# Moving loads, transposes and score bursts around in a fused attention and feed-forward kernel

## The chip, the cores and the metric

The kernel runs on one core of a Trainium2 chip. The metric is the device time of one execution in microseconds (us); lower is better. Before the change the median of 11 runs is 532.79 us (530.18 to 536.34).

## What is computed

For each of 8 batches and 12 heads, with 448 tokens and 64 features per head, an attention without softmax: the scaled scores are cut at zero, squared and divided by the length. The heads of a token are put side by side into a row x of 768 features. Each row is normalised (mean and variance over the row, a gain per feature), goes through two matrices with a cut at zero between them, and is added to x.

```python
scores = scale * np.matmul(q, k.transpose(0, 1, 3, 2))
attn = np.maximum(scores, 0.0) ** 2 / S
x = np.matmul(attn, v)                       # heads side by side: (8, 448, 768)
mu, var = x.mean(-1), ((x - mu) ** 2).mean(-1)
xn = (x - mu) / np.sqrt(var + 1e-06) * g_ln
out = x + np.maximum(xn @ w_ch1, 0.0) @ w_ch2    # 768 -> 3072 -> 768
```

## The kernel before

The order of all instructions on each engine is written out by hand (`tc.manual_schedule`): each engine works through its own list in program order, and semaphores between the lists keep data right. So an instruction that waits holds up all that follow it on its engine.

**Work items.** Heads go in pairs; pair i belongs to batch i // 6, so pairs 12 to 17 are batch 2. A pair's q and k are turned so that features lie on partitions: for batches 0 and 1 on TensorE (`pe_T`), for batches 2 to 7 by a transposing DMA (`att_T`, L253) out of a ring of three slots, `qk_ring`, which `load_qk` (L160) fills with three GpSimd-issued loads. `load_v` (L170) loads the values of two pairs. `att_QK` (L268) computes scores for 128 keys of both heads of a pair and cuts them at zero into a tile `at`; `att_square` (L294) squares them on VectorE. A pair has three such score steps. The last 64 keys of two neighbouring pairs are taken together in a fourth step of the even pair (t == NF, L279), which therefore reads the turned q and k of both pairs. `att_AV` (L304) multiplies by the values and evicts the result to `xT`, which has two halves of 448 columns, used by even and odd batches in turn; the eviction is on VectorE (L326), or, while FFN1 of batch 1 runs, on ScalarE (L324).

**Stages.** Batch 0's attention comes first (`step_fine`, `first_end`). Then, for each batch b: FFN1 (`ffn_1_all`: 24 columns of 128 hidden units, each 12 matmuls at L397 and a relu at L399 on ScalarE, with two PSUM banks in turn), then FFN2. FFN2 of batch 0 is plain (`ffn_2_first`, L442); the later ones form the product of 2 x 2 blocks from seven products with sums of blocks (`seven`, L459). The sums of weight blocks that this needs are made on VectorE (L210), some in FFN2 of batch 0 and the rest in FFN1 of batch 1.

**Bursts.** Between FFN1 columns of batch b stand the scores of batch b + 1: `excursion(3)` first multiplies a finished pair by its values, then issues three score steps. For batch 1 and on, these stand after the columns in `IN_REST` (1, 4, ... 19), and after column 22 the last pair is multiplied by its values. When a pair's last score step is issued, `queued` puts the transposing DMA of the pair three later on SyncE's queue, and notes the load of the pair six later.

**Normalisation.** The gain is applied to `xT` into `xc` (on ScalarE; for the first `GAIN_FIRST` parts of batch 0 on VectorE, L331), and the mean is taken off afterwards. For batch 0 the mean comes from `mean_part` (L340), six TensorE products with a matrix of -1/768; in `ffn_1_first` a part whose gain was applied on VectorE gets its mean with one VectorE instruction (`center_part`, L363), the others with an addition (L661) and a ScalarE scaling (L662). The division by the standard deviation is left to the end of FFN2.

**Tokens in rows.** For the residual addition and the variance, `ffn_x` (L373) copies x to `x_tok`, with tokens on partitions, by a transposing DMA for each sixth of the features. Tokens are taken in tiles of 128 over the batch borders: batch 0 has tiles 0 to 2, batch 1 tiles 3 to 6. Batch 1's transposes therefore start at column 384 of `xT`, 64 columns inside the half that batch 0 used and that batch 2 uses next. `ffn_stats` (L386) takes mean and variance of a tile on VectorE.

**Queues.** SyncE issues all transposing DMAs and all stores (L421), in program order. GpSimd issues all loads but the first few.

Of the kernel before, what the change touches and what calls it, by code (L numbers as in the profile page):

```python
# [11 lines left out]
def kernel(  # L12
# [29 lines left out]
    K1 = d_model // P  # L42
    K2 = d_ff // P
# [116 lines left out]
    def load_qk(i):  # L160
        b, a = divmod(i, NPAIR)
        ring = qk_ring[:, i % 3]
        q_to = ring[:SP, :NJ].rearrange("p j (x d) -> p j x d", x=2)
        k_to = ring[:, NJ:].rearrange("p t (x d) -> p t x d", x=2)
        heads = slice(2 * a, 2 * a + 2)
        nc.gpsimd.dma_start(q_to, q[b, heads].rearrange("x (p j) d -> p j x d", j=NJ))  # L166
        nc.gpsimd.dma_start(k_to[:, :NF], k[b, heads, :SF].rearrange("x (p t) d -> p t x d", t=NF))  # L167
        nc.gpsimd.dma_start(k_to[:SS, NF], k[b, 2 * a:2 * a + 2, SF:].rearrange("x s d -> s x d"))  # L168

    def load_v(i):  # L170

        b, a = divmod(i, NPAIR)
        v_heads, v_rest = v_parts(b)
        nc.gpsimd.dma_start(v_heads[:, 2 * a:2 * a + 4],
                            v[b, 2 * a:2 * a + 4, :SF].rearrange("h (p t) d -> p h (t d)", t=NF))
        for r0, h0, step in ((0, 0, 3), (D, 1, 1)):
            heads = slice(h0, h0 + step + 1, step)
            nc.gpsimd.dma_start(v_rest[r0:r0 + SS, a:a + 2, r0:r0 + D],  # L178
                                v[b, 2 * a:2 * a + 4][heads, SF:].rearrange("h s d -> s h d"))
# [88 lines left out]
    def att_QK(i, t, relu_by=nc.scalar):  # L268

        at = attn_pool.tile([P, 2, S], bf16, tag="attn")  # L270
        attn[i, t] = at
        ps = next_sc() if relu_by is nc.scalar else None
        half = [bank[:, :S] for bank in (spare if ps is None else (ps[:, 0], ps[:, 1]))]
        if t == NF:
            for x in range(2):
                for hh in range(2):
                    r = slice(hh * D, (hh + 1) * D)
                    r0 = row0(i + x, hh)
                    nc.tensor.matmul(by_j(half[x][r0:r0 + SS]), k_of(i + x, r, t, SS), q_of(i + x, r),  # L279
                                     start=True, stop=True)  # L280
        else:
            for hh in range(2):
                r = slice(hh * D, (hh + 1) * D)
                nc.tensor.matmul(by_j(half[hh]), k_of(i, r, t, P), q_of(i, r), start=True, stop=True)  # L284
        if ps is None:
            for x in range(2):
                if relu_by[x] is nc.scalar:
                    nc.scalar.activation(at[:, x], half[x], Act.Relu)
                else:
                    nc.vector.tensor_scalar(at[:, x], half[x], 0.0, None, op0=Alu.max)  # L290
        else:
            nc.scalar.activation(at, ps[:, :, :S], Act.Relu)  # L292
# [2 lines left out]
        nc.vector.tensor_mul(attn[i, t], attn[i, t], attn[i, t])  # L295


    GAIN_FIRST = 2
    av = {}

    def xT_of(b, ki):
# [2 lines left out]
    def att_AV(i, half=None, bank=None, evac_by=None):  # L304
# [24 lines left out]
        if b == 0:  # L329
            if pr < GAIN_FIRST:  # L330
                nc.vector.tensor_scalar(xc[:, pr, :], xT_of(b, pr), g_sb[:, pr:pr + 1], None, op0=Alu.mult)  # L331
# [7 lines left out]
    def mean_part(ki):  # L339
        nc.tensor.matmul(mean0, ones, xT_of(0, ki), start=(ki == 0), stop=(ki == K1 - 1))  # L340
# [218 lines left out]
    def warm_up(n):  # L559
        for _ in range(n):  # L560
            nc.tensor.matmul(spare[1][:, :256], ones, warm, start=True, stop=True)
# [47 lines left out]
    def step_fine(i):  # L609

        att_QK(i, 0)
        att_T(i + 1)
        att_square(i, 0)
        att_QK(i, 1)
        att_square(i, 1)
        if i:
            att_AV(i - 1, 0)
        else:
            warm_up(3)
        att_QK(i, 2)  # L620
        if i:
            att_AV(i - 1, 1)
        else:
            warm_up(3)
        att_square(i, 2)
        att_QK(i, NF)
        att_square(i, NF)
        if i:
            mean_part(i - 2)
            warm_up(1)  # L630
        else:
            warm_up(3)
        att_QK(i + 1, 0)
        if i:
            mean_part(i - 1)
        att_T(i + 2)
        att_square(i + 1, 0)
        att_QK(i + 1, 1)
        att_square(i + 1, 1)
        att_AV(i, 0)  # L640
        att_QK(i + 1, 2)
        att_AV(i, 1)
        att_square(i + 1, 2)

    def first_end():
        i = NPAIR
        att_AV(i - 1, 0)
        att_QK(i, 0)
        mean_part(i - 2)
        att_QK(i, 1)  # L650
        att_AV(i - 1, 1)
        mean_part(i - 1)

# [21 lines left out]
    T_IN_FIRST = {4: 1, 7: 2, 10: 3, 13: 4, 16: 5}  # L675
    X_AT = (4, 6, 8, 10, 12, 14)
    V_AT = {21: PE_T * NPAIR + 2, 23: PE_T * NPAIR + 4}
    STATS_AT = {0: (18, 21, 23), 1: (20, 21, 22, 23), 2: (6, 9, 12, 15)}
    IN_REST = (1, 4, 7, 10, 13, 16, 19)

    def ffn_1_all(b):
        ms = tiles_of(b)
        for ni in range(NI0 if b == 0 else 0, K2):
            if b == 0 and ni == NI0:
                ffn_1_first()
            if b < 2 and ni in X_AT:
                ffn_x(b, X_AT.index(ni))
            if b == 0 and ni in V_AT:
                load_v(V_AT[ni])
            ffn_1(ni)  # L690
            flush()
            at = STATS_AT[min(b, 2)][:len(ms)]
            if ni in at:
                ffn_stats(ms[at.index(ni)])
            if b == 1 and ni in SUMS_AT:
                w2_sums(*LATE_SUMS[SUMS_AT.index(ni)])
            if b == 0:
                if ni in IN_FIRST:
                    excursion(3)
                if ni == IN_FIRST[-1] + 3:  # L700
                    next_AV(bank=spare[1])
                if ni in T_IN_FIRST:
                    att_T(NPAIR + T_IN_FIRST[ni])
            elif b < B - 1:
                if ni in IN_REST:
                    excursion(3, **(dict(third=(nc.scalar, nc.vector), evac_by=nc.scalar) if b == 1 else {}))
                if ni == IN_REST[-1] + 3:
                    flush_loads()
                    next_AV(bank=spare[1])

# [5 lines left out]
    def ffn_2_first():  # L716
        b = 0
        ffn_rstd(b)
        box = {}
        assert not ready  # L720
        steps = center(1)
        n = 0
        for dh in range(2):

            order = [(m, part) for m in range(2) for part in range(4)]
            if dh:
                order.sort(key=lambda x: x[1] // 2)
            for m, part in order:
                plain_part(b, m, dh, part, 4, box)
                if n < K1 - 1:  # L730
                    gain(1, n)
                if n == 3:
                    gain(1, K1 - 1)
                if n in CENTER_AT:
                    steps[CENTER_AT.index(n)]()
                if n == 8:
                    carry(b)
                if n in (9, 10):
                    w2_sums(B_TOP, B11, B12, Alu.add, n - 9)
                if n in (12, 13):  # L740
                    w2_sums(B_SUM, B11, B22, Alu.add, n - 12)
                n += 1
# [33 lines left out]
    with tc.manual_schedule(engines=set(ENGINES)):  # L776
        load_heads(0, [("q", 2, 2), ("k", 2, 2), ("k last", 2, H - 2), ("q", 4, 4), ("k", 4, 4), ("v", 0, 4),
                       ("v last", 0, H), ("q", 8, 4), ("k", 8, 4), ("v", 4, 4), ("v", 8, 4)])
        load_early()
        load_heads(1, [("q", 0, 2), ("k", 0, 2), ("k last", 0, H)])  # L780
        load_w1(0)
        load_heads(1, [("q", 2, 4), ("k", 2, 4)])
        load_w1(1)
        load_w1(2)
        load_heads(1, [("v", 0, H), ("v last", 0, H), ("q", 6, 6), ("k", 6, 6)])
        for c in range(3, NCH):
            load_w1(c)
        warm_up(17)
        att_T(0)
        warm_up(5)  # L790
        for i in range(0, NPAIR, 2):
            step_fine(i)
        first_end()
        load_w2(B11, 0, 0)
        load_w2(B21, 1, 0)
        load_w2(B12, 0, 1)
        load_w2(B22, 1, 1)
        nc.gpsimd.memset(qk_ring, 0.0)
        i = PE_T * NPAIR
        load_qk(i)  # L800
        load_qk(i + 1)
        load_v(i)
        load_qk(i + 2)
        for b in range(B):
            ffn_1_all(b)
            if b == 0:
                ffn_2_first()
            else:
                ffn_2_all(b)
        flush()  # L810
# [30 lines left out]
```

## Time and profile before

| what | value |
|---|---|
| median of 11 runs | 532.79 us |
| profiled execution, its own time | 533.93 us |
| its span, first to last instruction | 532.2 us |
| granted TensorE clock, mean | 0.992 |
| TensorE matmuls (PE) busy | 519.9 us, 98% |
| VectorE (DVE) | 374.8 us, 70% |
| ScalarE (ACT) | 273.5 us, 51% |
| GpSimd (POOL) | 221.5 us, 42% |
| batch 0's attention | 4.7 to 28.3 us |
| FFN1 of batch 0 | 29.1 to 70.0 us |
| FFN2 of batch 0 | 70.0 to 86.0 us |
| FFN1 of batch 1 | 86.0 to 132.3 us |
| FFN1 of batch 2 | 160.0 to 197.8 us |

Times in the profile are counted from the first instruction. A busy share says how long an engine was at work, not that it held the others up; for that one reads who waited for whom. SP is SyncE, which only issues DMAs; the time from its issue to the landing of the data is given beside an issue's line. The granted clock is the share of full speed at which TensorE was allowed to run.

### The profile page before, as it was taken

Reading aid. Unit: us, or ns where it says so; the run is one execution under the profiler, and the core shown is the slowest. Engines: PE = TensorE matmul, PEld = TensorE weight load, DVE = VectorE, ACT = ScalarE, POOL = GpSimd, SP = SyncE. Lnnn points to the kernel's source line nnn. Section 1 sums busy time; section 2 is a strip of 40 time slices with the busy share of each in tenths; the row PEclk is TensorE's granted clock in tenths of the full one; section 3 lists DMA queues with packets and bytes.
Section 4 is the critical chain, followed back from the end, with each engine's and each line's share of the span. In section 5 each row is a group of like instructions: output and inputs, shape, how many; then the busy total and the mean of one; then the engine's idle time right before and its main releaser. Section 6 shows DMA issues by size and latency. Waiting matters only on the chain.

```text
span 532.2 us, 13700 instructions
## 1 busy us (share of the span) xinstructions
PE 519.9 (98%) x5707; PEld 315.1 (59%) x5707; DVE 374.8 (70%) x661; ACT 273.5 (51%) x445; POOL 221.5 (42%) x255
## 2 busy tenths in 40 slices
PE   8989999799999999999999999999999999999996
PEld 4345566355885556655566556655666556665665
DVE  5957779466876868669785787789685886951165
ACT  6965643566326663176632766376623666234320
POOL 8618116665433573425743256627732000320021
PEclk9999999889999999999999999999999999999999
DMA  9999999999534995549953599969914210240022
GB/s 141 175 186 205 203 198 122 193 124 120 51 82 91 106 115 51 105 95 111 98 66 89 91 104 105 127 76 106 115 46 108 53 21 2 59 115 10 1 60 61
DMA packets 175230, 53.04 MB, mean 100 GB/s; under 512 B 154176, under 2 KB 175168, under 8 KB 175168
## 3 DMA queue, kind: packets, MB, share of 16 engines
q0 software_dynamic: 103552, 25.74, 54.8%
q1 hardware_dynamic: 71088, 26.06, 27.6%
q8 instruction: 44, 0.72, 0.6%
q10 hardware_dynamic: 528, 0.37, 0.2%
q14 instruction: 18, 0.15, 0.1%
HBM read 51.91 MB, written 11.01 MB: 118 GB/s over the span
## 4 chain that ended last, share of the span: by engine, by line
PE 79%; DMA 12%; POOL 4%; DVE 2%; issue 1%; ACT 1%; POOLq 0%; ACTq 0%; DVEq 0%
PE f L397 35%; PE f L459 33%; DMA qk_ring<-in_q_dram 6%; PE f L319 5%; DMA s_sb<-in_v_dram 4%; PE sc L284 3%; DMA x_tok<-xT 2%; PE f L284 1%; DMA out_dram<-o_t 1%; POOL w L201 1%; DVE w L210 1%; POOL w L141 1%; POOL w L144 1%; PE sc L279 1%; POOL w L206 1%
## 5 line engine op out<-in xcount | busy, mean ns | idle before, releaser
L397 PE MATMUL f<-xc,w 128*64 128x448 bf16 x2256 | 229.8, 356 | 4.2 <-ACT xT L324 3.5
L397 PEld LDWEIGHTS <-w 128*64 128x64 bf16 x2256 | 125.9, 110 | 99.0 <-issue 23.3
L399 ACT ACTIVATE h<-f 128x448 bf16<-128x448 f32 x188 | 102.7, 546 | 104.6 <-PE f L397 103.1
L459 PE MATMUL f<-w,s_sb 128*64 128x384 bf16 (+2 forms) x1584 | 130.0, 324 | 0.0
L459 PEld LDWEIGHTS <-s_sb 128*64 128x64 bf16 x1584 | 92.3, 110 | 35.0
L292 ACT ACTIVATE at<-sc 128x896 bf16<-128x896 f32 x120 | 103.2, 916 | 16.0 <-PE sc L284 13.1
L295 DVE TENSOR_TENSOR at<-at 128x896 bf16<-128x896 bf16 x168 | 95.7, 616 | 10.1 <-ACT at L292 9.9
L493 POOL TENSOR_TENSOR o_t<-o_t,x_tok 128x384 f32<-128x384 f32 x26 | 24.4, 939 | 153.0 <-ACT o_t L492 138.6
L166 POOL DMA_DIRECT2D qk_ring<-in_q_dram x36 | 45.0, 1250 | 90.6 <-DMA qkT_t<-qk_ring 79.9
L290 DVE TENSOR_SCALAR at<-f 128x448 bf16<-128x448 f32 x89 | 51.5, 617 | 23.2 <-PE f L284 23.2
L453 DVE TENSOR_TENSOR s_sb<-h 128x1536 bf16<-128x1536 bf16 x65 | 64.8, 1013 | 0.0
L492 ACT ACTIVATE o_t<-f,rstd 128x384 f32<-128x384 f32 x26 | 15.1, 581 | 93.2 <-DVE acc L497 45.3
L167 POOL DMA_DIRECT2D qk_ring<-in_k_dram x36 | 53.7, 1492 | 4.6 <-DMA w<-in_moe_w_ch_dram 4.6
L459 PE MATMUL f<-w,h 128*64 128x384 bf16 x624 | 52.9, 326 | 0.0
L168 POOL DMA_DIRECT2D qk_ring<-in_k_dram x36 | 45.0, 1250 | 5.7 <-DMA w<-in_moe_w_ch_dram 5.7
L326 DVE TENSOR_SCALAR xT<-f 128x448 bf16<-128x448 f32 x43 | 26.7, 621 | 28.7 <-PE f L319 26.7
L459 PEld LDWEIGHTS <-h 128*64 128x64 bf16 x624 | 36.6, 110 | 14.4
L319 PE MATMUL f<-at,v_ring 128*64 128x448 bf16 x336 | 40.7, 359 | 0.2 <-DMA v_ring<-in_v_dram 0.2
L493 POOL TENSOR_TENSOR acc<-acc,x_tok 128x384 f32<-128x384 f32 x24 | 28.1, 1177 | 22.5 <-ACT acc L492 22.5
L178 POOL DMA_DIRECT2D v_ring<-in_v_dram x36 | 31.6, 1159 | 5.2 <-DMA w<-in_moe_w_ch_dram 5.0
L363 DVE SCALAR_TENSOR_TENSOR xc<-f,g_sb,xc 128x448 bf16<-128x448 f32 x44 | 27.9, 677 | 6.4 <-PE f L356 6.0
L284 PE MATMUL sc<-qkT_t 64*128 64x448 bf16 x206 | 31.5, 356 | 0.0
(81 smaller groups left out, 381.2 us busy)
## 6 DMA issues: line engine op xcount, KB each, us to landing
w<-in_moe_w_ch_dram POOLq DMA_DIRECT2D x6, 768.0 KB, 13.2
w<-in_moe_w_ch_dram POOLq DMA_DIRECT2D x4, 1152.0 KB, 26.7
v_ring<-in_v_dram POOLq DMA_DIRECT2D x21, 192.0 KB, 5.4
qk_ring<-in_q_dram POOLq DMA_DIRECT2D x36, 112.0 KB, 4.5
qk_ring<-in_k_dram POOLq DMA_DIRECT2D x36, 96.0 KB, 5.2
out_dram<-o_t SPq DMA_DIRECT2D x9, 168.0 KB, 2.2
out_dram<-o_t SPq DMA_DIRECT2D x9, 144.0 KB, 2.1
out_dram<-acc SPq DMA_DIRECT2D x7, 144.0 KB, 2.0
```

What stands on the lines that cost most here:

```text
L166: nc.gpsimd.dma_start(q_to, q[b, heads].rearrange("x (p j) d -> p j x d", j=NJ))
L167: nc.gpsimd.dma_start(k_to[:, :NF], k[b, heads, :SF].rearrange("x (p t) d -> p t x d", t=NF))
L284: nc.tensor.matmul(by_j(half[hh]), k_of(i, r, t, P), q_of(i, r), start=True, stop=True)
L290: nc.vector.tensor_scalar(at[:, x], half[x], 0.0, None, op0=Alu.max)
L292: nc.scalar.activation(at, ps[:, :, :S], Act.Relu)
L295: nc.vector.tensor_mul(attn[i, t], attn[i, t], attn[i, t])
L319: nc.tensor.matmul(ps[hh * D:(hh + 1) * D, :], weights, values, start=(n == 0), stop=(n == NF))
L397: nc.tensor.matmul(ps[c * D:(c + 1) * D, :], w1[:, ki, n0:n0 + D], xc[:, ki, :], start=(ki == 0), stop=(ki == K1 - 1))
L399: nc.scalar.activation(h[:, ni, CARRY:], ps, Act.Relu)
L453: nc.vector.tensor_tensor(s_sb[:, n], x, y, op=op)
L459: nc.tensor.matmul(ps[c * D:(c + 1) * D, :d1 - d0], stat[:, ki, c * D:(c + 1) * D], w2[:, slot, ki, d0:d1], start=(start and ki == 0), sto ...
L493: nc.gpsimd.tensor_tensor(o_t, o_t, x_half(m, dh), op=Alu.add)
```

## The change

The loads before the loop over the batches are put in another order: the q and k of pair 14 come ahead of the values of pairs 12 and 13. The six `x_tok` transposes of batch 1, which stood one by one in its FFN1 at columns 4, 6, ... 14, are now issued together in FFN2 of batch 0, after the third of its 16 pieces. The seven bursts in FFN1 of batch 1 stand two columns later (3, 6, ... 21), and the last product with the values after column 23 instead of 22. The token statistics of batch 1 stand at columns 15, 18, 21 and 23 instead of 20 to 23. In batch 0's attention the second mean product of a step moves from ahead of the q/k transposes to behind the last score step, the single warm-up matmul of each later step goes, two lines in `first_end` change places, and a third part gets its gain on VectorE.

```diff
-    GAIN_FIRST = 2
+    GAIN_FIRST = 3
...
             mean_part(i - 2)
-            warm_up(1)
         else:
             warm_up(3)
         att_QK(i + 1, 0)
-        if i:
-            mean_part(i - 1)
         att_T(i + 2)
...
         att_QK(i + 1, 2)
+        if i:
+            mean_part(i - 1)
         att_AV(i, 1)
...
         att_QK(i, 0)
+        att_QK(i, 1)
         mean_part(i - 2)
-        att_QK(i, 1)
         att_AV(i - 1, 1)
...
-    STATS_AT = {0: (18, 21, 23), 1: (20, 21, 22, 23), 2: (6, 9, 12, 15)}
+    STATS_AT = {0: (18, 21, 23), 1: (15, 18, 21, 23), 2: (6, 9, 12, 15)}
...
-            if b < 2 and ni in X_AT:
+            if b == 0 and ni in X_AT:
                 ffn_x(b, X_AT.index(ni))
...
             elif b < B - 1:
-                if ni in IN_REST:
+                shift = 2 if b == 1 else 0
+                if ni - shift in IN_REST:
                     excursion(3, **(dict(third=(nc.scalar, nc.vector), evac_by=nc.scalar) if b == 1 else {}))
-                if ni == IN_REST[-1] + 3:
+                if ni == min(IN_REST[-1] + shift + 3, K2 - 1):
                     flush_loads()
                     next_AV(bank=spare[1])
...
                     steps[CENTER_AT.index(n)]()
+                if n == 2:
+                    for ki in range(K1):
+                        ffn_x(1, ki)
                 if n == 8:
                     carry(b)
...
         load_qk(i)
         load_qk(i + 1)
+        load_qk(i + 2)
         load_v(i)
-        load_qk(i + 2)
```

## The prediction

> **What bounds the kernel now.** The times first: the median of the 11 runs is 532.79 us; the profiled execution took 533.93, of which its span is 532.2 and 1.7 lie around it. I make the sum against 533.93 and carry the difference in us over to the median. 0.5% (2.66 us) is about what a measurement of this kernel can tell from no change.
>
> Busy shares first: PE 98% of the span, so whatever isn't PE work counts only where PE waits for it. Then PE's list of waits, and ACT's between 86 and 132.4 us (waiter, line, releaser: us in total, times, longest).
>
> ```profile
> PE f L397 <- ACT xT L324: 3.5, 1, 3.5
> PE f L340 <- DVE xT L326: 1.4, 4, 0.7
> PE f L664 <- DVE xc L363: 0.8, 1, 0.8
> PE f L397 <- DVE o_t L428: 0.5, 1, 0.5
> ...
> ACT xT L324 <- DMA x_tok<-xT: 4.9, 1, 4.9
> ```
>
> All PE waits together are under 8 us, and one of them is 3.5. It lies in FFN1 of batch 1. PE's timeline there (start, us, instructions, idle before):
>
> ```profile
> 99.50 1.33 PE L397 MATMUL f<-xc,w 128*64 128x448 bf16 x12
> 104.31 4.94 PE L397 MATMUL f<-xc,w 128*64 128x448 bf16 x24 [3.49 <-ACT xT L324]
> 109.00 1.59 PE L319 MATMUL f<-at,v_ring 128*64 128x448 bf16 x8
> ```
>
> The wait is not all of the loss. 24 matmuls (two FFN1 columns) take 4.9 us afterwards, where batch 2 does the same in 2.46. The table of stretches gives the granted clock (fifth number):
>
> ```profile
> 102.50:104.30 1.80, 0.00 (x0) 0.77 1.13 175
> 104.30:109.00 4.70, 4.64 (x25) 0.50 2.11 177
> ...
> 110.40:112.00 1.60, 1.60 (x18) 1.00 1.09 70
> ```
>
> What PE waited for is in the chain of work that ended last, and in SP's queue, which issues every plain transpose and store:
>
> ```profile
> 90.52 4.89 DMA out_dram<-o_t
> 95.42 8.19 DMA x_tok<-xT
> ...
> 103.72 0.55 ACT xT L324
> ```
> ```profile
> 81.20 9.22 SPq L253 DMA_TRANSPOSE qkT_t<-qk_ring  x3
> 90.52 4.84 SPq L421 DMA_DIRECT2D out_dram<-o_t  x8
> 95.42 1.20 SPq L377 DMA_TRANSPOSE x_tok<-xT  x1
> 96.80 1.65 SPq L253 DMA_TRANSPOSE qkT_t<-qk_ring  x1
> ```
>
> ACT must evict pair 12's attention output (L324) into the half of xT that batch 0 used. Batch 1's tokens begin 64 columns inside that half, so the eviction waits until batch 1's first x transpose (L377) has read it. That transpose stands in SP's queue behind three qkT transposes and eight stores; it goes out at 95.42 and lands at 103.61. ACT is in order: the relu that frees PE's bank stands behind L324.
>
> To see what the stage should cost I take batch 2's FFN1, the same work without the wait. It runs from 160.02 to 197.76, 37.74 us. Batch 1's runs from 86.01 to 132.34, 46.33 us. The 8.59 us between them are: 3.49 wait; 4.90 - 2.27 = 2.63 for two columns at half clock (spacing from 104.31 to 109.26 in the chain, less its own micro-gaps); 1.33 - 0.76 = 0.57 for one AV product; 0.47 for L428 at column 1; about 1.4 for short ACT-paced gaps after each burst. Only the first three hang on the transposes: 6.7 us.
>
> **The change, part by part.**
>
> *Batch 1's six x transposes into FFN2 of batch 0.* On SP they now stand after the qkT transposes of pairs 12, 13, 14 and ahead of the eight stores; in FFN1 of batch 1 they leave the places between the later qkT transposes. Their source was complete at 71.83, when L326 ended. Pair 12's eviction now comes after the burst at column 9, at about 101. The first x transpose would be issued near 86.3 and land by 94.5 even with the longest latency seen (8.2). So the wait of 3.49 goes, with 5 us of cover, and its slow clock with it.
>
> How much the slow clock is worth is where a rule speaks against me. The trace: granted clock 0.50 from 103.46 to 110.29, cost 2.63 + 0.57 = 3.2. The Trainium skill, "TensorE: Matmul & The Clock Gate", Part 1, gives a warm-up of about 3.4 us of busy time at half rate, so it would charge 1.7 and the sum would be 3.49 + 1.7 = 5.2 instead of 6.7. I take the row, 3.2: it is this place's own.
>
> *Pair 14's q/k ahead of v.* POOL's issues in this stretch each wait for the load eight before them: v of pair 12 went out at 73.86, its rest at 79.63 and 80.48 (landed 83.8), then pair 14's q/k from 81.11 (landed 89.06). Swapped, pair 14 is issued at 73.86, 79.63 and 80.48 and lands between 84 and 86.5, say 85. Its qkT transpose then goes out at about 85 instead of 89.19: SP is free 4.2 us sooner. v of pair 12 comes by about 88; it is first used near 100. Nothing paid, nothing on PE's path by itself; it buys SP time.
>
> *Bursts two columns later.* Pure reordering on PE: the same seven bursts at columns 3, 6, ... 21. What matters is the fourth burst. Its first product (14, 3) reads the keys of pairs 14 and 15, so it needs pair 15's qkT transpose, which now stands behind six x transposes and eight stores.
>
> When PE needs it: column 1 starts at 87.80 as before (L428 is unchanged). Columns 1 to 3, 3 x 1.13: 91.19. Burst 0.67, three columns 3.83 (as after the first burst of before): 95.7. Burst 0.8, columns 3.58: 100.1. AV 0.88, burst 0.68, columns 3.65: 105.3. AV 0.88: 106.2.
>
> When it is there, by SP's issues: before, it was issued at 96.80 and landed at 104.27, 7.5 us later. Five x transposes more stand ahead of it (one did already). An issue takes 1.20 to 1.65 us in the rows around, one took 3.26; at 1.45 that is 7.3. Less the 4.2 of pair 14: 96.8 + 7.3 - 4.2 = 99.9, landed 107.4. By landings, a little later: in the built program each of SP's transfers waits for the one eight before it (before, the last store left at 95.04, when pair 14's transpose had landed at 95.03). Now the last store waits for the sixth x transpose: issued at 86.5 + 5 x 1.45 = 93.8, landed 6 to 7.5 later, 99.8 to 101.3; then the store, 0.4, and pair 15's transpose lands between 106.2 and 109.2. I take 107.7, the middle, since the load of transfers is then as before (share 1.6 to 1.9). From below, 1.24 an issue and 6 us a landing: 98.8 + 6.0 = 104.8, no wait. From above, two issues of 3.26 and pair 14's load at 86.5: 96.8 + 10.9 - 2.7 = 105.0, landed 112.5. So a new PE wait of about 1.5 us, charged at 1.5 since one so short left no slow clock elsewhere in the trace.
>
> The last AV follows the last burst by two columns instead of three. In before the third square of a burst ends 3.46 us after its start; two columns, burst and half an AV come to 3.5. I count 0.1.
>
> From (14, 3) on, before needed 132.34 - 110.51 = 21.83 us to the end of the stage; two columns fewer remain: 21.83 - 2.27 + 0.1 = 19.66. New end 107.7 + 19.66 = 127.36, gain 132.34 - 127.36 = 5.0 us. After that PE runs without a wait to the end in the profile, so the gain reaches the end.
>
> *Token statistics spread (L388 to L390), 15, 18, 21, 23.* 1.13 us of DVE each, in gaps of 1.2 to 2.4 us that DVE has after the bursts; it reads what landed by about 101, column 15 is at about 110. Nothing; if the gaps closed, the squares behind it would be late by 1.13 at one burst.
>
> *Mean products later, two warm-up matmuls gone, a third gain on DVE.* PE would save 0.27 + 0.18 + 2 x 0.2 in the two steps. But DVE is busy 12.83 of the 13 us from 13 to 26, so it paces that stretch, and the third L331 adds 0.3 to it. In the first FFN1 columns the third part no longer goes over ACT: the gap before it (30.89 against 30.57) goes, 0.3. Net between -0.3 and +0.8; +0.2 by the rows. It isn't in the sum: the loads fix pair 15's time, so PE would only wait longer for it.
>
> **Sum.** 533.93 - 5.0 = 528.9 for the profiled execution; on the median, 532.79 - 5.0 = 527.8.
>
> **The rivals.**
>
> *No new wait (0.18).* Pair 15 lands before 106.2. For it: transposes at 152 to 160 us landed 2.3 us after issue. Against: those had a transfer share of 0.35, here it is above 1.5. Gain 132.34 - (106.2 + 19.66) = 6.5, up to 7.3 with the early part: 525.5 to 526.3.
>
> *A longer wait without the slow clock (0.17).* Pair 15 at 108.5 to 109.5; gain 3.2 to 4.2, 528.6 to 529.6. It joins the likeliest case at its edge.
>
> *The new wait takes the place of the old one, and slower (0.15 for a wait beyond 3 us).* Nine transposes stand in a row on SP, among POOL's loads of pairs 15, 16 and v. If issues of 3.26 are the rule there, pair 15 lands after 110. PE then idles over 3.3 us at the fourth burst and pays the slow clock again, 3.2. Break-even is a wait of 6.5 - 3.2 = 3.3, pair 15 at 109.5. At 112.5 it is 6.3 + 3.2 - 6.5 = 3.0 slower, 535.8. Against: pair 14's earlier landing lets three x transposes go out in 85 to 92, where the share falls to 0.84 between 88 and 92.
>
> *The eviction waits all the same (0.05).* It would if the first x transpose landed after 101. Then only the rest is left: 531.5 to 533. The 5 us of cover speak against it.
>
> **How the numbers follow.** The likeliest case, a new wait of 0.4 to 2.3 us, has 0.45: 526.7 to 528.6, at 527.8. The range takes in the whole of the longer wait and the eviction case and leaves out the half of the slower rival that is really slower (0.08) and the best of the no-wait case (some 0.08): 525.6 to 532.5. Faster by over 0.5% (below 530.1): 0.45 + 0.18 + 0.17, less 0.02 for a tail: 0.78. Slower (above 535.5): about half of the 0.15, 0.08. Within: 0.14.
>
> **What would show it.** Right: no PE wait on L324 in FFN1 of batch 1, granted clock 1.0 throughout it, the first x transpose on SP near 86, the stage some 40 to 41 us long. A PE wait at the fourth burst's L279, released by pair 15's qkT transpose, of about 1.5 us; none would mean the first rival, over 3 us with a clock of 0.5 after it the third. Wrong it would be if SP's transposes slow each other, or if moved traffic delays the loads of pairs 15 and 16 past 100.

## The result

The changed kernel takes 528.14 us (median of 12 runs, 527.09 to 530.27); the kernel before, measured again beside it, 533.99 us (47 runs). The ratio is 0.9902, 95% interval 0.9879 to 0.9925: 5.2 us less of 533.99, where 5.0 was forecast (the medians themselves lie 5.9 us apart). The profiled execution has a span of 526.4 us (532.2 before) and took 528.14.

TensorE's waits over the whole span, changed kernel (waiter, line, releaser: us in total, times, longest), then ScalarE's wait for transfers between 84 and 132 us:

```profile
PE f L561 <- DVE w L101: 1.2, 1, 1.2
PE f L340 <- DVE xT L326: 0.9, 2, 0.7
PE f L663 <- DVE xc L363: 0.8, 1, 0.8
PE f L397 <- DVE o_t L428: 0.7, 2, 0.5
...
```
```profile
ACT xT L324 <- DMA out_dram<-o_t: 0.2, 1, 0.2
```

The 1.2 us of L561 lie at the start of both kernels. The 3.5 us on L324 are gone from TensorE's list, and of ScalarE's 4.9 us 0.2 are left. SyncE's queue, changed kernel (start, length of the issues, what):

```profile
82.34 5.79 SPq L253 DMA_TRANSPOSE qkT_t<-qk_ring  x3
88.18 7.83 SPq L377 DMA_TRANSPOSE x_tok<-xT  x6
96.10 5.39 SPq L421 DMA_DIRECT2D out_dram<-o_t  x8
102.38 3.80 SPq L253 DMA_TRANSPOSE qkT_t<-qk_ring  x2
```

The first x transpose leaves at 88.18 (95.42 before) and lands at 92.65, 9 us before pair 12's eviction at 101.95. Pair 15's transpose now leaves at 102.38 (96.80 before) and lands at 107.33. TensorE's timeline at the fourth burst, which needs it, and the granted clock (third number from the end of a stretch's row):

```profile
106.17 0.95 PE L319 MATMUL f<-at,v_ring 128*64 128x448 bf16 x8
107.05 0.69 PE L279 MATMUL sc<-qkT_t 64*64 64x448 bf16 x4
107.68 0.36 PE L284 MATMUL sc<-qkT_t 64*128 64x448 bf16 x2
```
```profile
95.00:105.00 10.00, 9.86 (x98) 5.16 (x94) 7.64 (x12) 7.98 (x14) 5.56 (x8) 1.00 1.78 197
...
107.00:112.00 5.00, 5.00 (x52) 2.71 (x52) 3.97 (x9) 3.89 (x8) 4.10 (x6) 1.00 0.92 105
```

The four products of L279 take 0.69 us where a burst that waits for nothing takes 0.38: the third of them reads pair 15 and started some 0.3 us late. The clock stays at 1.00. FFN1 of batch 1 runs from 86.75 to 126.58, 39.83 us, against 46.33 before.

### The profile page after: what moved, and what is told of

It is laid out like the page before. It is cut to its first block, busy times and chain, and to the rows that moved or that the text cites. A ratio compares the mean times of both kernels' runs of the same rounds, so it can differ in the third digit from the quotient of the medians.

```text
span 526.4 us, 13704 instructions
## 1 busy us (share of the span) xinstructions
PE 518.0 (98%) x5705; PEld 310.5 (59%) x5705; DVE 376.2 (71%) x662; ACT 273.0 (52%) x444; POOL 221.7 (42%) x255
## 4 chain that ended last, share of the span: by engine, by line
PE 79%; DMA 12%; POOL 3%; DVE 2%; issue 1%; ACT 1%; SPq 0%; POOLq 0%; DVEq 0%; ACTq 0%
PE f L397 35%; PE f L459 34%; DMA w<-in_moe_w_ch_dram 6%; PE f L319 5%; DMA s_sb<-in_v_dram 4%; PE sc L284 3%; PE f L284 1%; DMA w<-in_q_dram 1%; DVE w L210 1%; DMA out_dram<-o_t 1%; POOL w L201 1%; PE sc L279 1%; ACT at L292 1%; POOL w L144 1%; PE f L356 0%
## 5 line engine op out<-in xcount | busy, mean ns | idle before, releaser
L397 PE MATMUL f<-xc,w 128*64 128x448 bf16 x2256 | 226.8, 354 | 0.9 <-DVE o_t L428 0.7
L397 PEld LDWEIGHTS <-w 128*64 128x64 bf16 x2256 | 124.6, 110 | 94.7 <-issue 19.3
L459 PEld LDWEIGHTS <-s_sb 128*64 128x64 bf16 x1584 | 89.7, 110 | 37.6
L166 POOL DMA_DIRECT2D qk_ring<-in_q_dram x36 | 47.7, 1324 | 92.2 <-DMA qkT_t<-qk_ring 82.5
L167 POOL DMA_DIRECT2D qk_ring<-in_k_dram x36 | 56.5, 1570 | 9.6 <-DMA w<-in_moe_w_ch_dram 9.6
L168 POOL DMA_DIRECT2D qk_ring<-in_k_dram x36 | 46.6, 1294 | 5.5 <-DMA w<-in_moe_w_ch_dram 5.5
```

Of the source, the lines that this page charges most:

```text
L397: nc.tensor.matmul(ps[c * D:(c + 1) * D, :], w1[:, ki, n0:n0 + D], xc[:, ki, :], start=(ki == 0), stop=(ki == K1 - 1))
L459: nc.tensor.matmul(ps[c * D:(c + 1) * D, :d1 - d0], stat[:, ki, c * D:(c + 1) * D], w2[:, slot, ki, d0:d1], start=(start and ki == 0), sto ...
```

## The experiments

The question was which edit carries the gain, and how much of the old loss was the wait itself and how much the slow clock. "Stage" is FFN1 of batch 1 in the profiled execution, from its first product to the first of FFN2.

| run | ratio to before | stage, us |
|---|---|---|
| before | 1 | 46.33 |
| the change | 0.9902 (0.9879 to 0.9925) | 39.83 |
| later bursts alone | 0.9914 (0.9894 to 0.9935) | 41.89 |
| early transposes alone | 1.0001 (0.9976 to 1.0026) | 46.21 |
| change, bursts not later | 0.9976 (0.9947 to 1.0006) | 41.73 |
| change, v loaded first | 0.9954 (0.9927 to 0.9982) | 39.94 |
| attention edits alone | 1.0002 (0.9969 to 1.0036) | 45.52 |
| before, 36 fillers | 0.9995 (0.9969 to 1.0021) | 46.64 |
| before, 116 fillers | 0.9980 (0.9958 to 1.0002) | 44.53 |
| split version | 0.9887 (0.9854 to 0.9921) | 38.97 |
| split version, again | 0.9904 (0.9874 to 0.9934) | 38.98 |
| the change, again | 0.9927 (0.9899 to 0.9955) | 39.68 |
| later bursts and weight sum | 0.9970 (0.9941 to 1.0000) | 40.77 |

Each kernel was timed on the same chip as runs of the kernel before, which the runs of one group share. The first group is later bursts, early transposes, bursts not later and 36 fillers; the second is v first, attention edits, 116 fillers and split version; the third is the last three rows. The kernel before has medians of 534.06, 533.85 and 531.48 us in them. What differs is how often its clock fell: 4 of 29, 4 of 29 and 11 of 26 runs kept a mean clock of 0.998 or more. In all three groups such runs have a median of 530.3 to 530.5 us and the others 533.9 to 534.2. So a ratio of the third group is not to be set beside one of the others.

### Later bursts alone

```diff
-                if ni in IN_REST:
+                shift = 2 if b == 1 else 0
+                if ni - shift in IN_REST:
...
-                if ni == IN_REST[-1] + 3:
+                if ni == min(IN_REST[-1] + shift + 3, K2 - 1):
```

> The kernel before with the bursts of batch 1's FFN1 two columns later and nothing else. Theory A (the gain comes from ending pair 12's wait, by whichever means): the x transposes stay where they were, the first lands at 103.6, and pair 12's eviction comes up only at about 101.8 instead of 98.8; ScalarE then waits 1.8 us instead of 4.9, TensorE at most 0.5, the clock stays at 1.0; gain about 6 us, ratio 0.988 to 0.991, as much as the whole change. Theory B (the transposes must move for a gain): ScalarE's wait stays near 4.9 or grows, ratio 0.998 to 1.002.

Measured 529.21 us, ratio 0.9914. TensorE's and ScalarE's waits in the stage:

```profile
PE f L397 <- ACT h L399: 1.2, 1, 1.2
...
PE f L397 <- ACT xT L324: 1.0, 1, 1.0
```
```profile
ACT xT L324 <- DMA x_tok<-xT: 2.4, 1, 2.4
```

The x transposes are still issued in FFN1 of batch 1 (the first at 96.76, landed at 104.54), and most of the gain is there: the eviction comes up two columns later and waits 2.4 us instead of 4.9 (1.8 was expected), TensorE 1.0 + 1.2 in two pieces (at most 0.5 was expected). In all six timed runs the granted clock was 1.00. That is theory A, a little short of its ratio; the transposes need not move for a gain. How firm it is, a later run shows (below): the same idea gave less.

### Early transposes alone

```diff
-            if b < 2 and ni in X_AT:
+            if b == 0 and ni in X_AT:
...
+                if n == 2:
+                    for ki in range(K1):
+                        ffn_x(1, ki)
```

> The kernel before with batch 1's x transposes moved into FFN2 of batch 0 and nothing else. Theory A (moving them trades the wait on pair 12's eviction for one on pair 15's transpose): pair 14's transpose leaves at about 89, so pair 15's lands near 110, while the fourth burst, now at column 10, wants it at about 104; TensorE waits near 6 us there and the clock falls to half after it; 0 to 3 us slower than before, ratio 1.000 to 1.006. Theory B (the transposes alone carry the gain): no wait over 1 us, ratio 0.988 to 0.991.

Measured 533.93 us, ratio 1.0001. TensorE's timeline and the clock behind it:

```profile
103.92 0.38 PE L279 MATMUL sc<-qkT_t 64*64 64x448 bf16 x2
107.98 0.58 PE L279 MATMUL sc<-qkT_t 64*64 64x448 bf16 x2 [3.68 <-DMA qkT_t<-qk_ring]
```
```profile
106.50:113.20 6.70, 5.22 (x28) 2.21 (x30) 3.50 (x5) 2.71 (x4) 4.69 (x7) 0.50 0.99 131
```

ScalarE waits for no x transpose any more, and TensorE waits 3.7 us for pair 15's transpose instead, behind six x transposes and eight stores, with the same slow clock after it. The wait moved from one reader of SyncE's queue to the next. Theory A, though the wait is 3.7 and not 6 us: pair 15 landed at 107.94, not at 110. None of its 12 timed runs kept a mean clock of 0.998.

### The change without the later bursts, and without the load order

```diff
-                shift = 2 if b == 1 else 0
+                shift = 0
```

> The changed kernel with the bursts back at columns 1, 4, ... 19. Theory A: pair 15's transpose lands at about 107.3 and the fourth burst wants it at about 104.8; TensorE waits 2.5 us there; ratio to before 0.993 to 0.996 if the clock stays at 1.0, 0.998 to 1.001 if it falls. Theory B (the shift is idle reordering once the transposes are early): ratio 0.989 to 0.991.

Measured 533.01 us, ratio 0.9976. The profiled execution kept its clock:

```profile
PE sc L279 <- DMA qkT_t<-qk_ring: 1.6, 1, 1.6
```

It took 530.76; 9 of the 12 timed runs had a mean granted clock under 0.998, and their median is 533.3. So theory A with the clock falling more often than not; the wait was 1.6 us where 2.5 was expected, and the ratio lies between the two that were given for a clock that stays and one that falls. Undoing the shift costs 4 us of the 5.2.

```diff
-        load_qk(i + 2)
         load_v(i)
+        load_qk(i + 2)
```

> The changed kernel with v of pairs 12 and 13 loaded ahead of pair 14's q and k again. Theory A (pair 14's place in the loads sets when SyncE's queue gets free): pair 14's transpose leaves at about 89.5 instead of 86.5, pair 15's lands near 110 and the fourth burst wants it at 107; TensorE waits 2 to 3 us there, in some runs with slow clock after it; ratio to before 0.994 to 0.999. Theory B (the load order is hidden): no such wait, ratio 0.989 to 0.992.

Measured 531.14 us, ratio 0.9954: 2.8 us of the gain lost (0.0052 of 534). Pair 14's transpose left at 89.82 and pair 15's landed at 108.87, 1.5 us later than in the changed kernel:

```profile
108.48 0.80 PE L279 MATMUL sc<-qkT_t 64*64 64x448 bf16 x4
```

In the profiled execution little of it is seen as a wait (0.80 us, 0.4 over 0.38), because TensorE itself had come to this stage 1.4 us late, at 88.18. Why is in the last section: its clock had fallen at 29 us (it was 0.42 us ahead of the changed kernel at 29.23 and 1.01 behind at 35.44). At the changed kernel's pace the wait would have been about 1.8 us (108.87 less 107.05). The ratio is theory A's; its wait of 2 to 3 us was not seen. That the lost 2.8 us are this wait and what it does to the clock is inferred from these times: 8 of the 12 timed runs had a mean clock under 0.998, and the one that was profiled had lost it at 29 us, not here.

### The attention edits alone

The third gain on VectorE, the later mean products, the missing warm-up products and the exchanged lines of `first_end`, on the kernel before.

> The kernel before with the edits of batch 0's attention alone (third gain on VectorE, later mean products, no single warm-ups). Theory A (VectorE paces that stretch): ratio 0.999 to 1.001, the first FFN1 product 0.2 us earlier at most, the 4.9 us wait of ScalarE for the x transpose unchanged. Theory B (these edits carry part of the gain): ratio 0.997 or below.

Measured 533.21 us, ratio 1.0002. That is theory A's ratio. In its profile the first TensorE product with values comes 0.05 us later than before (11.21 against 11.16, before any of these edits has acted), and the first burst of FFN1 0.26 us earlier (33.75 against 34.01); so the edits gave 0.3 us. The changed kernel says the same: 0.73 us later (11.89), then 0.42 us later (34.43).

One thing came out otherwise than expected. The wait for the x transpose was to stay at 4.9 us, and this profile has

```profile
PE f L397 <- ACT xT L324: 1.9, 1, 1.9
```
```profile
ACT xT L324 <- DMA x_tok<-xT: 3.4, 1, 3.4
```

The first x transpose left at 94.60 and landed at 101.71, 1.9 us earlier than in the profile of before, with nothing edited in this stage. So the same wait is longer in one execution and shorter in another. TensorE waited 1.9 and then 1.2 us for ScalarE, and the clock was at half for 6.83 us all the same.

### TensorE kept busy during the old wait

Small products (64 columns, into a part of a PSUM bank that nothing reads) ahead of column 9, in the kernel before. First 36 of them.

```diff
+            if b == 1 and ni == 9:
+                for _ in range(36):
+                    nc.tensor.matmul(spare[1][:, S:], ones, ones[:, :512 - S], start=True, stop=True)
             ffn_1(ni)
```

> The kernel before with 36 extra small matmuls (64 columns, into a part of a PSUM bank that nothing reads) ahead of column 9 of batch 1's FFN1, so that TensorE is at work during its 3.5 us wait; the wait itself stays. Theory A (3.2 us of the loss are the slow clock that the idle stretch brings): granted clock 1.0 after the wait, ratio 0.993 to 0.996. Theory B (the slow clock follows from something else in this stage, or the wait alone is the loss): clock 0.5 as before, ratio 0.999 to 1.003.

Measured 532.73 us, ratio 0.9995: theory B's number, but not conclusive. The fillers took 1.2 us in all, so TensorE still idled 2.9 and then 1.2 us, and the clock fell for 3.4 us. The same with 116:

> As the run with 36 small matmuls, with 116: one took 34 ns there, so these fill 3.9 us, the whole of the wait of column 9, and their results are read by nothing. Theory A (the slow clock comes from the idle stretch): ScalarE's wait for the x transpose stays at 4 to 5.5 us, granted clock 1.0 in the profile, time like the runs of before that kept a clock of 1.0 (529.5 to 530.7 us); ratio 0.992 to 0.995. Theory B: the clock falls all the same, ratio 0.998 to 1.003.

Measured 532.73 us, ratio 0.9980. TensorE's timeline, ScalarE's wait, and the clock:

```profile
100.64 3.06 PE L692 MATMUL f<-ones 128*128 128x64 bf16 x99
103.97 0.66 PE L692 MATMUL f<-ones 128*128 128x64 bf16 x17 [0.27 <-issue]
104.56 1.33 PE L397 MATMUL f<-xc,w 128*64 128x448 bf16 x12
106.65 1.33 PE L397 MATMUL f<-xc,w 128*64 128x448 bf16 x12 [0.77 <-ACT h L399]
```
```profile
ACT xT L324 <- DMA x_tok<-xT: 4.9, 1, 4.9
```
```profile
104.60:110.00 5.40, 4.63 (x47) 2.51 (x48) 3.71 (x6) 4.21 (x8) 2.84 (x3) 1.00 1.90 137
```

ScalarE waits 4.9 us as in the kernel before, and the clock is 1.00 throughout: the slow clock does come from the idle stretch, which was theory A. But it is worth less than I charged, and the ratio of 0.992 to 0.995 was missed (3 of the 12 timed runs also had a mean clock under 0.998). The stage takes 44.53 us against 46.33, 1.8 us, and the timed runs 1.1 (0 to 2.2). The fourth line above says why: at full speed TensorE is through its column sooner and then waits 0.77 us for ScalarE, which is still working off the relus that stood behind the eviction. Part of the slow clock lay over that backlog. The fillers end 0.3 us past the old wait (104.56 against 104.31, in a stage that starts 0.05 earlier), so in the profile the slow clock is worth about 2.1 us. The timed runs say less; a likely reason is that the fillers always take their 3.9 us, while the old wait is shorter in some executions (as in the profile of the attention edits alone). That is not shown for the timed runs.

### A split version, and both kernels once more

If pair 15's transpose is the tightest thing left, three of the six x transposes can stand behind it. One weight sum (L210) was also put behind L428, for which column 1 waits 0.5 us.

```diff
             elif b < B - 1:
+                if b == 1 and ni in (7, 8, 9):
+                    ffn_x(1, ni - 4)
...
-                    for ki in range(K1):
+                    for ki in range(3):
                         ffn_x(1, ki)
...
-                if n in (12, 13):
-                    w2_sums(B_SUM, B11, B22, Alu.add, n - 12)
+                if n in (12, 15):
+                    w2_sums(B_SUM, B11, B22, Alu.add, (n - 12) // 3)
```

> The changed kernel with only three x transposes in FFN2 of batch 0 and the other three after columns 7, 8 and 9 of batch 1's FFN1, behind pair 15's transpose on SyncE, and with the second half of one weight sum put behind the last store's addition (L428) on VectorE. Theory A (pair 15's transpose is the tightest thing left, and stands behind six x transposes): it leaves 3.7 us earlier, at 98 to 99, lands by 105, no TensorE wait over 0.3 us in this stage; L428's wait at column 1 (0.5 us) goes; 0.5 to 1.2 us below the changed kernel, ratio to before 0.986 to 0.990. Theory B (nothing is tight any more): the changed kernel's 0.990, within 0.001.

Measured 527.18 us, ratio 0.9887. TensorE has no wait at all in this stage; the fourth burst:

```profile
105.99 0.38 PE L279 MATMUL sc<-qkT_t 64*64 64x448 bf16 x4
```

Pair 15's transpose left at 95.93 and landed at 105.38. To compare it with the changed kernel on one chip, both were run again, and with them the later bursts with that weight sum and nothing else:

> The changed kernel itself, on one chip with the next two. Theory A (its last tight place, pair 15's transpose, makes some runs wait): ratio to before 0.989 to 0.992, its runs spread over 2 to 3 us, some with a granted clock of 0.997. Theory B (nothing is tight): as narrow as the split version's runs.

> The split version again (three x transposes behind pair 15's, one weight sum behind L428). Theory A: 0.5 to 1.5 us below the changed kernel beside it, runs within 2 us of each other, clock 1.0 in nearly all. Theory B: the same as the changed kernel within 0.3 us.

> The kernel before with the bursts two columns later and the second half of one weight sum behind L428, the x transposes and loads left as they were. Theory A (the later bursts carry most of the gain, and the 0.5 us of L428 comes off as well): ratio to before 0.989 to 0.992, ScalarE still waits 1 to 3 us for the first x transpose. Theory B (a column that starts 0.5 us earlier only waits 0.5 us longer for that transpose): as the run with the later bursts alone, 0.991 to 0.993.

The changed kernel: 528.04 us, ratio 0.9927 (0.9899 to 0.9955). The split version: 527.19 us, 0.9904 (0.9874 to 0.9934). It is 0.85 us lower in the medians, and 0.96 when both groups of runs are put together (527.18 against 528.14); the intervals overlap, so this is a difference that the profiles explain (0.2 to 0.3 us at L279, 0.5 to 0.7 at L428) rather than a proven gain. Its runs are not narrower (526.26 to 528.41 against 527.5 to 529.04), and 4 of 10 had a clock under 0.998, against 2 of 11: on that, theory A was wrong. The changed kernel's ratio of 0.989 to 0.992 was missed too, though its own median moved by only 0.1 us; what moved is the kernel before.

The later bursts with the weight sum: 530.85 us, 0.9970 (0.9941 to 1.0000), less than the later bursts alone had given. Its profile looks the same (ScalarE waits 1.9 us for the first x transpose, TensorE 0.5 and 1.2), but 7 of its 12 runs had a clock under 0.998, where none of the six of the earlier run had. Put together, the 11 runs of both at full clock have a median of 529.2 and the 7 others of 531.5. So the later bursts alone give 1.6 us by the one ratio and 4.6 by the other: of these 3 us, 2.6 are the lower median of before in this group and the rest is how often the leftover wait costs the clock. Against the changed kernel's 528.1 the two medians are 1.1 and 2.8 us longer. Theory A's ratio was missed, and theory B's too.

## Why the prediction was right

**The wait.** Batch 1's x transposes moved, the wait of 3.49 us on L324 went, and the slow clock after it. The first x transpose left at 88.18 where 86.3 was said, mostly since pair 14's q and k landed at 86.24 and not at 85; the cover was 9 us at the eviction, where 5 was said.

**Pair 15.** This was the step that decided the size. Said: leaves at 100 to 101.7, lands at 107.7. Measured: 102.38 and 107.33. Said: TensorE wants it at 106.2 and waits 1.5. Measured: wanted at 107.05, waited 0.3, just under the 0.4 to 2.3 of the likeliest case. Of the difference, 0.4 is the earlier landing, and 0.74 is the start of the stage, later by that much than in the profile of before: 0.42 was there at the first burst of batch 0's FFN1, the rest came in FFN2 of batch 0, 0.19 of it as a wait for L428. In this sum the transfers do not shift with TensorE, so a late start only made the wait shorter; that the sum tied both to absolute times is its weak point.

**The end of the stage.** Said 127.36, measured 126.58: pair 15 landed 0.4 us sooner, and from there to the end of the stage it took 19.25 us where 19.66 was said. Said some 40 to 41 us long, measured 39.83. From there to the end no wait took the gain back: 5.76 us at the end of the stage, 5.8 in the span.

**The slow clock.** The 3.2 us were read from the row as the price of the clock, and as that they were too much. From the end of the wait to the fourth burst the kernel before needs 6.20 us (104.31 to 110.51), and with the wait filled and the clock kept up 4.10 (104.56 to 108.66): the clock alone is about 2.1, and most of the rest is ScalarE's backlog (the 0.77 us above). As what goes with the wait the 3.2 were about right, since the backlog goes too: the stage is 6.50 us shorter although 0.3 at L279 and 0.2 at L428 are new, 7.0 in all, against the 6.7 that were put down. The forecast of 5.0 does not rest on it in any case: it is the landing of pair 15 plus the work behind it. Only the charge of the slower rival does. The Trainium skill's figure ("TensorE: Matmul & The Clock Gate", Part 1) would have made it 1.7, an estimate, nearer to the 2.1; but its 3.4 us of work at half rate are not what this trace has: TensorE was back at work at 104.31 and at half clock until 110.29, 5.98 us.

**Where luck came in.** The sum was made for one execution and carried over to the median. That held because the profiled execution, 533.93 us, was near the median of 533.99. Between runs at full clock the change is worth 2.7 us (last section), so a profile of such a run need not have given 5.0.

**What the sum left unsaid.** I called the later bursts a pure reordering. The 106.2 had them in it, but they relax both deadlines on SyncE's queue by two columns, 2.3 us: pair 12's eviction as well as pair 15's transpose. The transposes alone gain nothing (1.0001), and taking the later bursts out of the change costs 4 us. The rival "the new wait takes the place of the old one" is what the early transposes do without them and without the new order of loads, at 3.7 us and with the slow clock.

**The attention edits** were counted at nothing (+0.2 by the rows): 1.0002. The statistics spread over the stage and the last AV one column closer showed no wait of TensorE; neither was run alone.

## What to carry to other kernels

When one queue feeds several readers in order, moving one transfer forward moves the others back: write down for each reader behind it when it wants its data and when that lands, before and after. Shifting the readers by a column or two may do as much as shifting the transfers, and with both the waits were shorter than with either alone. A profile gives the landing times of its own execution: in four profiles with the same queue order (before, attention edits, both fillers) the first x transpose landed anywhere from 101.71 to 104.55. Whether a wait of 1 to 4 us also costs the clock differs from run to run too, so compare the clock of all timed runs, of the kernel before as well, and not only the medians.

## What the runs showed of the hardware

The kernel before is spread over 529.3 to 537.6 us, and its granted clock goes with it. Of the 84 runs that stand beside these experiments, 19 had a mean clock of 0.998 or more, with a median of 530.4 us; the other 65 had a median of 534.1. Of the changed kernel's 23 runs, 17 kept that clock, with a median of 527.7, and the 6 others have 528.9. So between runs at full clock 2.7 us lie, and the rest of the 5.2 goes with the clock falling less often and for less long. The two can't be taken apart further: the kernel before with its wait filled kept the clock in 9 of 12 runs and took 532.7, 2.3 us more than its own full-clock runs, which the 0.3 us of overshoot doesn't explain; so the runs of before at full clock may be those in which the transfers came sooner. No profile of such a run was taken.

The slow stretches come in steps: 3.41 us in two of the profiled executions, 6.83 in three (103.46 to 110.29 before, and the same length in the runs with the early transposes alone and with the attention edits alone). The times between are steps too. From the first full clock to the fall it is 98.99 us before (4.47 to 103.46), 102.40 with the early transposes alone and 23.89 with v first: 29, 30 and 7 times 3.413 us. So one can cut an execution into windows of 3.413 us from its first full clock on, and read TensorE's busy time in the window that ended when the clock fell, and in the first slow one:

| run | window | TensorE busy, us | first slow window | slow for, us |
|---|---|---|---|---|
| before | 100.05 to 103.46 | 0.77 | 2.52 | 6.83 |
| early transposes alone | 103.03 to 106.45 | 1.27 | 1.88 | 6.83 |
| before, 36 fillers | 103.96 to 107.37 | 1.32 | 3.05 | 3.41 |
| attention edits alone | 100.29 to 103.71 | 1.51 | 2.25 | 6.83 |
| change, v loaded first | 25.62 to 29.04 | 1.92 | 3.22 | 3.41 |

The clock came back after one window where TensorE was busy for over 3 us of it, and after two where it was not. In all 13 profiles no window with more than 1.92 us was followed by a fall (the end of the span left out). Nine windows have 1.78 to 1.93 us, and after one of them the clock fell; in the changed kernel 27.64 to 31.06 has 1.93 and the clock stayed up. This would explain why a wait costs the clock in some runs only: the first window begins anywhere from 3.98 to 7.23 us, so a wait falls into one window or is divided over two. With the later bursts alone the 1.0 and 1.2 us fell into two, with 2.46 and 2.25 us busy, and the clock held. For the timed runs it is not shown.

It needs no single long wait. In the run with v loaded first the clock fell at 29.04 us, after waits of 0.2 and 0.7 us and within a third of 0.8:

```profile
26.48 0.35 PE L340 MATMUL f<-xT,ones 128*128 128x448 bf16 x1 [0.20 <-DVE xT L326]
...
28.11 0.35 PE L340 MATMUL f<-xT,ones 128*128 128x448 bf16 x1 [0.71 <-DVE xT L326]
29.23 1.28 PE L663 MATMUL f<-xc,w 128*128 128x448 bf16 x3 [0.78 <-DVE xc L363]
```
```profile
26.00:29.00 3.00, 1.54 (x10) 0.53 (x7) 2.09 (x4) 1.73 (x2) 1.43 (x2) 1.00 1.26 202
29.10:32.40 3.30, 3.17 (x9) 1.32 (x9) 3.30 (x7) 1.47 (x3) 0.10 (x1) 0.50 1.23 197
```

TensorE was at work for only 1.54 of 3.00 us there. The same three waits stand in the changed kernel's profile, 0.4 us later, and its clock stayed up. My remark that so short a wait had left no slow clock in the trace was true of that trace, and no rule. What decides between the two, at 1.92 and 1.93 us in their windows, these runs do not settle.
